# Attention's set-up copies move to the start, and the softmax sums and the product's copies move from VectorE to ScalarE

## The chip, the cores and the metric

The kernel runs on one core of a Trainium2 chip. A core has five engines that work side by side: TensorE (PE in the rows; its weight loads are PEld), VectorE (DVE), ScalarE (ACT), GpSimd (POOL) and SyncE (SP), which issues most of the transfers. Each engine takes its own instructions in order. The metric is the device time of one execution in microseconds, the median of several runs; lower is better. A profile shows a single execution.

## The reference

An attention over 4 batches of 8 heads feeds a mixture of experts (one expert for each token), and that feeds a gated product. Only the attention and the hand-over to the experts matter here.

```python
q_rot, k_rot = rotate(q), rotate(k)                 # 4 x 8 heads, 576 positions, 64 wide
scores = matmul(q_rot, k_rot^T) / 8
attn = exp(scores - max(scores))
attn = attn / (sum(attn) + 1e-9)
x = (attn @ v) -> [2304 tokens, 512]
logits = x @ w_gate                                  # chooses each token's expert
eom = sigmoid(x @ w_output_gate)
# then: experts with w1, w2; then gate * value @ w_out
```

## The kernel before

The 32 heads are taken as 16 pairs (g = 0 to 15), and the 576 queries of a pair in five pieces (j = 0 to 4, the last with 64 queries of both heads). One step t = 5g + j of the main loop writes out, for every engine in this order:

- scores(g, j): TensorE's products of queries and keys (L279, for j = 4 L274), VectorE's two negated row maxima (L285, tile nm), and ScalarE's two exponentials (L292, tile p), each followed by a short instruction that reads the row sum out of its accumulator. For j = 4 there is one maximum and one exponential.
- pv of step t-2: the product with the values (L339, L347) into the PSUM tile o. After j = 1 and j = 4 parts of o are copied to SBUF, to oT (256 columns after j = 1; 256 and 64 columns after j = 4). As pv runs two steps behind, the copies for j = 1 come in a step with j = 3, and those for j = 4 in a step with j = 1 of the next pair.
- turn_last and turn of step t-1: TensorE transposes the exponentials (L310, L325), VectorE copies one block (L311, tile pt), and ScalarE copies two pieces of 512 columns (L328, tile pt). The next step's pv reads pt.
- in steps with j = 3 and j = 4, xf(g-1): TensorE turns oT back to rows by a product with wI (L382). wI holds an identity matrix and beside it the two gates' weights, so that each row also gets its gate logits. VectorE divides by the softmax sum (L392 to L402). The sum of the last 64 queries, which lie in the two halves of the partitions, is brought together by a small product with the matrix fold (L390).
- for j = 0 to 2, tqk of the next pair: the transposes of its keys and queries (L241, L249), whose high and low parts VectorE writes (L230, L231). In pair 0's own set-up ScalarE writes the high parts (L228).

All transposes, xf's products and tqk's share three PSUM tiles (pool pst), and the scores two pairs of tiles (pool pss). A tile is free for its next user when its last reader is done. GpSimd rotates the pair after next (L193 to L208); of the first pair VectorE does it. In step 2 late_setup, and at the end of step 5 late_setup2, set up what xf and the choice of experts need: wI, fold, ones, tri, ids_tok and base.

Ahead of the loop the kernel turns the first pair's keys and queries. In the wait for them TensorE runs transposes of the identity whose results nobody reads ("spin", L221): 30 ahead of the keys' own and 8 ahead of the queries'.

Of the kernel before, what the change touches and what calls it, by code (L numbers as in the profile page):

```python
# [9 lines left out]
F32 = mybir.dt.float32  # L10
# [4 lines left out]
AF = mybir.ActivationFunctionType  # L15
ALU = mybir.AluOpType
# [27 lines left out]
XW = DM + 1  # L44
EPS = 1e-9
# [20 lines left out]
def tile_kernel(  # L66
# [16 lines left out]
    nc = tc.nc  # L83
# [38 lines left out]
    halves = mc[:, 280:282]  # L122
# [57 lines left out]
    rotd = {}  # L180
# [30 lines left out]

        return a, b

    def tqk(g, eng=nc.vector, spin=(0, 0, 0)):

        i = g % 2

        def place(n):
            ps = pst.tile([128, 512], F32, tag="t", name="t")
            for _ in range(spin[n]):  # L220
                nc.tensor.transpose(ps[:, 0:128], idf, idf)  # L221
            return ps

        def halves_of(hi, lo, ps, nm):

            f = SCALE if nm == "q" else 1.0
            if eng is nc.scalar:
                nc.scalar.activation(out=hi, in_=ps, func=AF.Copy, scale=f)  # L228
            else:
                nc.vector.tensor_scalar(out=hi, in0=ps, scalar1=f, scalar2=None, op0=ALU.mult)  # L230
            nc.vector.scalar_tensor_tensor(  # L231
                out=lo, in0=ps, scalar=f, in1=hi.bitcast(F32), op0=ALU.mult, op1=ALU.subtract
            )

        def main(nm):
            def f():
                src = rotd[g, nm]
                h, l = qT[i] if nm == "q" else (t[:, 64:576] for t in kT[i])
                ps = place("kq".index(nm))
                for c in range(4):  # L240
                    nc.tensor.transpose(ps[:, 128 * c : 128 * c + 128], src[:, c, :], idf)  # L241
                halves_of(h, l, ps, nm)

            return f

        def tails():
            ps = place(2)
            for n, nm in enumerate("kq"):
                nc.tensor.transpose(ps[:, 64 * n : 64 * n + 64], rotd.pop((g, nm))[0:64, 4, :], idf[0:64, 0:64])  # L249
            for c in (0, 576):  # L250
                halves_of(*(t[:, c : c + 64] for t in kT[i]), ps[:, 0:64], "k")
            for e in range(2):
                r = slice(64 * e, 64 * e + 64)
                halves_of(*(t[r, r] for t in qD[i]), ps[r, 64:128], "q")

        return [main("k"), main("q"), tails]

# [74 lines left out]
    def pv(g, j):  # L332
        if j == 0:
            OPS[g] = po.tile([128, 512], F32, tag="o", name="o")
        ps, src, (va, vd) = OPS[g], PT.pop((g, j)), vraw[g]
        q0, n = (128 * j, 128) if j < 4 else (0, 64)
        for c in range(4):
            for e in range(2):
                nc.tensor.matmul(  # L339
                    ps[64 * e : 64 * e + 64, q0 : q0 + n],  # L340
                    va[:, e, c, :],
                    src[:, 4 * e + c, :] if j < 4 else src[:, c, 64 * e : 64 * e + 64],
                    start=(c == 0),
                    stop=False,
                    skip_group_check=True,
                )
        nc.tensor.matmul(ps[:, q0 : q0 + n], vd, src[:, 8, 0:n], start=False, stop=True, skip_group_check=True)  # L347
        if j == 1:
            nc.vector.tensor_copy(O[g % 2][:, 0:256], ps[:, 0:256])
        elif j == 4:  # L350
            nc.vector.tensor_copy(O[g % 2][:, 256:512], ps[:, 256:512])
            nc.vector.tensor_copy(O[g % 2][:, 512:576], ps[:, 0:64])

# [9 lines left out]
    def xf(g):  # L365
# [4 lines left out]
        def part(c0, nch):  # L370
            def f():
                if c0 == 0:
                    st["r"] = sm.tile([128, 5, 2], F32, tag="r", name="r")
                    st["x"] = xp.tile([128, 5, 129], F32, tag="x", name="x")
                    sp = sm.tile([128, 2], F32, tag="sp", name="sp")
                    nc.vector.tensor_tensor(out=sp, in0=halves, in1=lst.pop(g).to_broadcast([128, 2]), op=ALU.mult)
                    st["sp"] = sp
                X, r = st["x"], st["r"][:, c0 : c0 + nch, :]
                ps = pst.tile([128, 512], F32, tag="t", name="t")
                for c in range(nch):  # L380
                    cc = c0 + c
                    nc.tensor.matmul(  # L382
                        ps[:, 160 * c : 160 * c + 160],
                        O[g % 2][:, 128 * cc : 128 * cc + 128],
                        wI[:, h, :],
                        start=True,
                        stop=True,
                    )
                if c0:
                    nc.tensor.matmul(ps[:, 320:322], fold, st["sp"], start=True, stop=True)  # L390
                    nc.vector.tensor_copy(l[:, 4, :], ps[:, 320:322])
                nc.vector.tensor_scalar(out=r, in0=l[:, c0 : c0 + nch, :], scalar1=EPS, scalar2=None, op0=ALU.add)  # L392
                nc.vector.reciprocal(out=r, in_=r)
                r = r.unsqueeze(3)
                pv_ = ps[:, 0 : 160 * nch].rearrange("p (c w) -> p c w", w=160)
                nc.vector.tensor_tensor(
# [587 lines left out]
        nc.vector.memset(t, 1.0)  # L984
    for t in (*(x.bitcast(F32) for x in (*qD[0], *qD[1])), *(vd for _, vd in vring + vlast)):
        nc.vector.memset(t, 0.0)
    load(1)
    load(0, "v")
    R = {nm: rot(0, nm) for nm in "kq"}
    for nm in "kq":  # L990
        for f in R[nm]:
            f(eng=nc.vector)
    first, gate_q = tqk(0, nc.scalar, (30, 8, 0)), rotd[0, "q"]
    for f in first:
        f()

    nc.gpsimd.tensor_copy(scr, gate_q[0:1, 0, 0:1])
    load(2)
# [4 lines left out]

    def late_setup():
        nc.sync.dma_start(out=mc, in_=misc)
        nc.gpsimd.memset(wI, 0.0)
        nc.gpsimd.memset(pinit, DUMMY)
        for t in O:
            nc.gpsimd.memset(t[:, 576:640], 0.0)
        nc.sync.dma_start(out=x_dram[0:1, :], in_=wI.rearrange("p h w -> p (h w)")[0:1, 0:XW])  # L1010
        for e in range(2):
            r = slice(64 * e, 64 * e + 64)
            for o, w in ((0, w_gate), (E, w_og)):
                c = 128 + 16 * e + o
                nc.sync.dma_start(
                    out=wI[r, :, c : c + E],
                    in_=w.rearrange("(h e p) n -> e p h n", h=4, e=2)[e],
                )

    def late_setup2():  # L1020
        nc.vector.tensor_copy(wI[:, :, 0:128], idf.unsqueeze(1).to_broadcast([128, 4, 128]))
        nc.vector.tensor_copy(tri, mc[:, 0:128])
        for o in range(2):
            nc.vector.tensor_tensor(
                out=fold[:, 64 * o : 64 * o + 64], in0=idf[:, 0:64], in1=idf[:, 64:128], op=ALU.add
            )
        nc.vector.memset(ones, 1.0)
        nc.vector.tensor_copy(ids_tok, mc[:, 128:148])
        nc.vector.tensor_copy(base, mc[:, 272:280])
        nc.sync.dma_start(out=perm_dram.rearrange("(p a) o -> p (a o)", p=128), in_=pinit)  # L1030

    M["seq"] = MAIN
# [9 lines left out]
    for t in range(NJ * NPAIR):  # L1042
        g, j = divmod(t, NJ)
        if t == NJ * (NPAIR - 1):
# [6 lines left out]
            gather(0)  # L1051
            gather(1)
        scores(g, j)
        if t >= 2:
            pv(*divmod(t - 2, NJ))
        if t >= 1:
# [316 lines left out]
```

## Time and profile before

| | before |
|---|---|
| median of 3 runs | 1128.62 us (1127.61 to 1129.76) |
| profiled execution | 1129.55 us, of which the span from first to last instruction is 1127.8 us |
| busy share of the span | PE 95%, PEld 85%, DVE 68%, ACT 52%, POOL 32% |
| TensorE clock granted, mean | 0.986 of full speed |
| attention's steps | from about 11 to 360 us |

A row of a timeline begins with the start and the duration in us, then engine, line of the kernel, operation, output<-input with the partitions and elements, the count, and in brackets how long the engine had been idle and what released it.

### The profile page before, as it was taken

The page shows a single profiled execution, that of the slowest core. Times are in us where ns is not written, and L with a number is a line of the kernel's source. Part 1 is how long each engine was busy: PE and PEld are TensorE (multiplying, and loading weights), DVE is VectorE, ACT ScalarE, POOL GpSimd, SP SyncE. Part 2 cuts the span into 40 slices and gives each one's busy share as a digit, 9 for nine tenths or more (in the row PEclk, how much of TensorE's full clock was granted, in tenths as well). Part 3 has the DMA queues.
Part 4 walks back from the last instruction along what each step waited for, and adds up shares of the span by engine and source line. Part 5 has one row for each costly group of instructions (what it writes and reads, how often), then busy time and mean ns, then how long its engine had stood idle before and what let it go on. Part 6 is the DMA issues. An engine that isn't in the chain of part 4 may idle for free. (4 is left out here: it accounts for less than half of the span.)

```text
span 1127.8 us, 20456 instructions
## 1 busy us (share of the span) xinstructions
PE 1076.3 (95%) x7682; PEld 961.7 (85%) x7682; DVE 771.9 (68%) x1439; ACT 582.2 (52%) x1122; POOL 360.3 (32%) x336
## 2 busy tenths in 40 slices
PE   7799998989998999999999999999999999999998
PEld 6688787778777988988888889888999999999997
DVE  6778787787876886889989868854444545444442
ACT  4466455555544344667667656654444444444432
POOL 6335454553612103444333134521111111111111
PEclk8899999999999999999999999999999999999999
DMA  4144045045008297699999543300010010100000
GB/s 112 37 84 77 12 50 102 9 56 87 30 14 227 48 146 267 197 330 301 324 302 318 200 142 122 103 1 28 1 57 1 10 47 1 57 1 1 28 1 28
DMA packets 97053, 111.61 MB, mean 99 GB/s; under 512 B 16817, under 2 KB 75441, under 8 KB 96946
## 3 DMA queue, kind: packets, MB, share of 16 engines
q1 hardware_dynamic: 92482, 97.81, 31.2%
q0 software_dynamic: 4320, 12.08, 3.7%
q8 instruction: 62, 1.02, 0.4%
q14 instruction: 45, 0.37, 0.1%
q10 hardware_dynamic: 144, 0.33, 0.1%
HBM read 103.03 MB, written 15.56 MB: 105 GB/s over the span
## 5 line engine op out<-in xcount | busy, mean ns | idle before, releaser
L1242 POOL TENSOR_TENSOR gl<-gf,gh 128x384 fp32r<-128x384 f32 x72 | 73.3, 1018 | 348.6 <-ACT gh L1241 348.6
L292 ACT ACTIVATE p<-s,nm 128x576 f32<-128x576 f32 x144 | 105.6, 738 | 125.8 <-DVE nm L285 121.4
L771 DVE TENSOR_TENSOR lo<-wr,hi 128x1024 fp32r<-128x1024 f32 x112 | 156.4, 1409 | 14.7 <-ACT hi L770 14.3
L1237 DVE TENSOR_TENSOR gf<-v,sg 128x384 f32<-128x384 f32 x72 | 40.0, 555 | 134.0 <-PE v L1233 134.0
L285 DVE TENSOR_REDUCE nm<-s 128x1 f32<-128x576 f32 x144 | 102.9, 751 | 39.2 <-PE s L279 26.0
L1241 ACT CAST gh<-gf 128x384 fp32r<-128x384 f32 x72 | 36.9, 513 | 160.5 <-DVE gf L1237 160.5
L1216 DVE TENSOR_TENSOR gl<-gw,gh 128x512 fp32r<-128x512 f32 x72 | 72.9, 1012 | 66.8 <-ACT gh L1215 66.7
L770 ACT CAST hi<-wr 128x1024 fp32r<-128x1024 f32 x106 | 109.7, 1052 | 5.4 <-PE y L861 2.7
L325 PE MATMUL t<-idf,p 128*128 128x128 f32 x576 | 84.4, 282 | 19.0 <-DVE pt L311 16.7
L1231 PE MATMUL t<-yh,gh 128*128 128x384 f32 x288 | 99.1, 344 | 1.8 <-ACT gh L1215 1.6
L1233 PE MATMUL t<-yh,gl 128*128 128x384 f32 x288 | 97.4, 338 | 0.6 <-DVE gl L1216 0.2
L1232 PE MATMUL t<-yl,gh 128*128 128x384 f32 x288 | 96.7, 336 | 0.0
L1233 PE MATMUL v<-yh,vl 128*128 128x384 f32 x288 | 96.2, 334 | 0.0
L1231 PE MATMUL v<-yh,vh 128*128 128x384 f32 x288 | 96.2, 334 | 0.0
L1232 PE MATMUL v<-yl,vh 128*128 128x384 f32 x288 | 96.2, 334 | 0.0
L328 ACT COPY pt<-t 128x512 f32<-128x512 f32 x144 | 79.2, 589 | 31.3 <-PE t L325 30.7
L325 PEld LDWEIGHTS t<-idf,p 128*128 128x128 f32 x576 | 67.1, 146 | 27.1 <-DVE pt L311 21.3
L830 PE MATMUL h<-xl,hi 128*128 128x256 f32 x288 | 82.0, 285 | 1.8 <-DVE sc L806 1.8
L830 PE MATMUL h<-xh,hi 128*128 128x256 f32 x288 | 81.9, 284 | 0.7 <-DVE hl L835 0.7
L830 PE MATMUL h<-xh,lo 128*128 128x256 f32 x288 | 81.5, 283 | 0.0
L1235 ACT ACTIVATE sg<-t 128x384 f32<-128x384 f32 x72 | 35.3, 491 | 81.8 <-PE t L1233 81.8
L861 PE MATMUL y<-hi,hl 128*128 128x512 f32 x184 | 73.0, 397 | 4.6 <-DVE hl L847 4.4
(235 smaller groups left out, 2974.8 us busy)
## 6 DMA issues: line engine op xcount, KB each, us to landing
wr<-in_moe_w_dram SPq DMA_DIRECT2D x112, 512.0 KB
cv<-in_moe_w_gate_dram SPq DMA_DIRECT2D x12, 512.0 KB
cv<-in_moe_w_val_dram SPq DMA_DIRECT2D x12, 512.0 KB
cv<-in_moe_w_out_dram SPq DMA_DIRECT2D x12, 512.0 KB
yt<-y_dram SPq DMA_DIRECT2D x18, 256.0 KB
out_dram<-ob SPq DMA_DIRECT2D x18, 256.0 KB
kraw<-in_k_dram SPq DMA_DIRECT2D x16, 256.0 KB
qraw<-in_q_dram SPq DMA_DIRECT2D x16, 256.0 KB
```

Source lines behind the costliest of these rows:

```text
L285: nc.vector.tensor_reduce(out=nm, in_=s[:, :, 0:288], axis=AX.XY, op=ALU.max, negate=True)
L292: nc.scalar.activation(out=P[g, j][:, e, :].rearrange("p (a b) -> p a b", a=2), in_=s[:, :, 0:288], func=AF.Exp, bias=nm, scale=1.0, accum ...
L325: nc.tensor.transpose(ps[:, 128 * c : 128 * c + 128], src[:, e, k0 + 128 * c : k0 + 128 * c + 128], idf)
L328: nc.scalar.copy(dst[:, 4 * e : 4 * e + 4, :].rearrange("p c q -> p (c q)"), ps)
L770: nc.scalar.copy(out=hi, in_=t)
L771: nc.vector.tensor_tensor(out=lo, in0=t, in1=hi.bitcast(F32), op=ALU.subtract)
L830: nc.tensor.matmul(ps[:, c, :], w[:, kk, 128 * c : 128 * c + 128], x[:, kk, :], start=first, stop=last)
L861: nc.tensor.matmul(ps, hl, rh, start=False, stop=False)
L1231: nc.tensor.matmul(ps[:, 0:TG], wh[:, c], yh[:, kk, :], start=(kk == 0), stop=False)
L1232: nc.tensor.matmul(ps[:, 0:TG], wh[:, c], yl[:, kk, :], start=False, stop=False)
L1233: nc.tensor.matmul(ps[:, 0:TG], wl[:, c], yh[:, kk, :], start=False, stop=(kk == KD - 1))
L1242: nc.gpsimd.tensor_tensor(out=gl, in0=gf, in1=gh.bitcast(F32), op=ALU.subtract)
```

## The change

1. wI's identity and zero columns and the matrix fold are made by VectorE ahead of the loop, behind its first memsets. late_setup2 keeps three copies out of mc (tri, ids_tok, base), now by ScalarE, and ones, now by GpSimd.
2. The first pair's set-up is reordered: the 64-column remainder ("tails") of the keys is turned behind the keys' main part, and that of the queries only after scores(0, 0). The dummy transposes are 30, 6 and 0, and 14 ahead of the queries' remainder.
3. The three copies of o to oT go from VectorE to ScalarE in every pair.
4. In xf, ScalarE makes sp (from the last sums) and writes the sums plus EPS into spare columns of the PSUM tile that the product with wI fills; VectorE takes the reciprocal from there. A multiplication, two additions and a copy leave VectorE for each pair, and a sum no longer goes by way of lsum.
5. The row of zeros at the head of x_dram is written from pinit by 27 partitions, no longer from wI.

```diff
@@ tqk @@
-    def tqk(g, eng=nc.vector, spin=(0, 0, 0)):
+    def tqk(g, eng=nc.vector, spin=(0, 0, 0, 0)):
...
-        def tails():
-            ps = place(2)
+        def tails(which="kq"):
+            ps = place(2 if "k" in which else 3)
             for n, nm in enumerate("kq"):
+                if nm not in which:
+                    continue
                 nc.tensor.transpose(ps[:, 64 * n : 64 * n + 64], rotd.pop((g, nm))[0:64, 4, :], idf[0:64, 0:64])
...
@@ pv @@
         if j == 1:
-            nc.vector.tensor_copy(O[g % 2][:, 0:256], ps[:, 0:256])
+            nc.scalar.copy(O[g % 2][:, 0:256], ps[:, 0:256])
         elif j == 4:
-            nc.vector.tensor_copy(O[g % 2][:, 256:512], ps[:, 256:512])
-            nc.vector.tensor_copy(O[g % 2][:, 512:576], ps[:, 0:64])
+            nc.scalar.copy(O[g % 2][:, 256:512], ps[:, 256:512])
+            nc.scalar.copy(O[g % 2][:, 512:576], ps[:, 0:64])
@@ xf @@
-                    nc.vector.tensor_tensor(out=sp, in0=halves, in1=lst.pop(g).to_broadcast([128, 2]), op=ALU.mult)
+                    nc.scalar.activation(out=sp, in_=halves, func=AF.Copy, scale=lst.pop(g))
...
+                e = ps[:, 480 : 480 + 2 * nch]
                 if c0:
                     nc.tensor.matmul(ps[:, 320:322], fold, st["sp"], start=True, stop=True)
-                    nc.vector.tensor_copy(l[:, 4, :], ps[:, 320:322])
-                nc.vector.tensor_scalar(out=r, in0=l[:, c0 : c0 + nch, :], scalar1=EPS, scalar2=None, op0=ALU.add)
-                nc.vector.reciprocal(out=r, in_=r)
+                    nc.scalar.activation(out=e[:, 0:2], in_=l[:, 3, :], func=AF.Copy, bias=EPS)
+                    nc.scalar.activation(out=e[:, 2:4], in_=ps[:, 320:322], func=AF.Copy, bias=EPS)
+                else:
+                    nc.scalar.activation(out=e.rearrange("p (c h) -> p c h", h=2), in_=l[:, 0:3, :], func=AF.Copy, bias=EPS)
+                nc.vector.reciprocal(out=r, in_=e.rearrange("p (c h) -> p c h", h=2))
@@ ahead of the loop @@
+    nc.vector.memset(wI[:, :, 128:160], 0.0)
+    nc.vector.tensor_copy(wI[:, :, 0:128], idf.unsqueeze(1).to_broadcast([128, 4, 128]))
+    for o in range(2):
+        nc.vector.tensor_tensor(out=fold[:, 64 * o : 64 * o + 64], in0=idf[:, 0:64], in1=idf[:, 64:128], op=ALU.add)
...
-    first, gate_q = tqk(0, nc.scalar, (30, 8, 0)), rotd[0, "q"]
-    for f in first:
-        f()
+    first, gate_q = tqk(0, nc.scalar, (30, 6, 0, 14)), rotd[0, "q"]
+    first[0]()
+    first[2]("k")
+    first[1]()
@@ late_setup @@
-        nc.gpsimd.memset(wI, 0.0)
...
-        nc.sync.dma_start(out=x_dram[0:1, :], in_=wI.rearrange("p h w -> p (h w)")[0:1, 0:XW])
+        nc.sync.dma_start(out=x_dram[0:1, :].rearrange("o (p c) -> (o p) c", p=27), in_=pinit[0:27, 0:19].bitcast(F32))
@@ late_setup2 @@
-        nc.vector.tensor_copy(wI[:, :, 0:128], idf.unsqueeze(1).to_broadcast([128, 4, 128]))
-        nc.vector.tensor_copy(tri, mc[:, 0:128])
-        for o in range(2):
...
-        nc.vector.memset(ones, 1.0)
-        nc.vector.tensor_copy(ids_tok, mc[:, 128:148])
-        nc.vector.tensor_copy(base, mc[:, 272:280])
+        nc.gpsimd.memset(ones, 1.0)
+        for o, c in ((tri, slice(0, 128)), (ids_tok, slice(128, 148)), (base, slice(272, 280))):
+            nc.scalar.copy(out=o, in_=mc[:, c])
@@ main loop @@
         scores(g, j)
+        if t == 0:
+            first[2]("q")
         if t >= 2:
             pv(*divmod(t - 2, NJ))
```

In the three places below the lines of the changed kernel are other numbers for the same code: L279 became L283, L285 L289, L292 L296, L311 L315, L328 L332, L349 to L352 became L353 to L356.

VectorE's list around the end of step 5 before (tile nm is the maximum, oT the copied product):

```order
L231 SCALAR_TENSOR_TENSOR kTl_150<-t,kTh_149 128x512
L1021 COPY wI<-idf 128x4x128
L1022 CAST tri<-mc 128x128
L1024 TENSOR_TENSOR fold<-idf 128x64 x2
L1027 MEMSET ones 128x128
L1028 CAST ids_tok<-mc 128x20
L1029 COPY base<-mc 128x8
L285 TENSOR_REDUCE nm<-s 128x1 x2
L351 COPY oT_154<-o 128x256
L352 COPY oT_154<-o 128x64
L311 COPY pt<-t 128x128
```

and the same place now:

```order
L231 SCALAR_TENSOR_TENSOR kTl_150<-t,kTh_149 128x512
L289 TENSOR_REDUCE nm<-s 128x1 x2
L315 COPY pt<-t 128x128
L230 TENSOR_SCALAR qTh_141<-t 128x512
L231 SCALAR_TENSOR_TENSOR qTl_142<-t,qTh_141 128x512
```

The six set-up rows and the two copies of oT are gone from between step 6's inputs and its maxima, and from between the maxima and the copy of pt.

ScalarE's list from a step with j = 1 to the next step with j = 4, in pair 2, before:

```order
L292 ACTIVATE p,lsum_156<-s,nm 128x576 x2
L328 COPY pt<-t 128x512 x2
L292 ACTIVATE p,lsum_156<-s,nm 128x576 x2
L328 COPY pt<-t 128x512 x2
L292 ACTIVATE p,lsum_156<-s,nm 128x576 x2
L328 COPY pt<-t 128x512 x2
L292 ACTIVATE p,lst<-s,nm 128x576
L328 COPY pt<-t 128x512 x2
```

and now, from behind the exponentials of the step with j = 1:

```order
L355 COPY oT_155<-o 128x256
L356 COPY oT_155<-o 128x64
L332 COPY pt<-t 128x512 x2
L296 ACTIVATE p,lsum_156<-s,nm 128x576 x2
L332 COPY pt<-t 128x512 x2
L296 ACTIVATE p,lsum_156<-s,nm 128x576 x2
L353 COPY oT_154<-o 128x256
L380 ACTIVATE sp<-mc,lst 128x2
L400 ACTIVATE t<-lsum_156 128x6
L332 COPY pt<-t 128x512 x2
L296 ACTIVATE p,lst<-s,nm 128x576
L397 ACTIVATE t<-lsum_156 128x2
```

Two copies (j = 1), a copy and two small activations (j = 3) and two small activations (j = 4; the second, L398, is the next row) now stand between the exponentials and the two copies of pt.

TensorE's list at the program's start, before:

```order
L221 MATMUL t<-idf 128x128 x30
L241 MATMUL t<-idf,trk 128x128 x4
L221 MATMUL t<-idf 128x128 x8
L241 MATMUL t<-idf,trq 128x128 x4
L249 MATMUL t<-idf,trk 128x64
L249 MATMUL t<-idf,trq 128x64
L279 MATMUL s<-kTh_149,qTh_141 128x288 x2
```

and now:

```order
L221 MATMUL t<-idf 128x128 x30
L241 MATMUL t<-idf,trk 128x128 x4
L251 MATMUL t<-idf,trk 128x64
L221 MATMUL t<-idf 128x128 x6
L241 MATMUL t<-idf,trq 128x128 x4
L283 MATMUL s<-kTh_149,qTh_141 128x288 x2
```

and, also now, at the end of the first step's scores and the beginning of the second's:

```order
L283 MATMUL s<-kTh_149,qTl_142 128x288 x2
L283 MATMUL s<-kTl_150,qTh_141 128x288 x2
L221 MATMUL t<-idf 128x128 x14
L251 MATMUL t<-idf,trq 128x64
L283 MATMUL s<-kTh_149,qTh_141 128x288 x2
```

The keys' remainder comes ahead of the queries' wait, and the 14 dummy transposes with the queries' remainder stand between the first and the second step's scores.

## Rows read from the trace of the kernel before

**Rows 1.** Windows: PE, PEld, DVE, ACT, POOL busy us (instructions), clock, DMA share, GB/s.
```profile
50.00:100.00 50.00, 49.59 (x538) 43.00 (x537) 38.58 (x103) 30.10 (x69) 18.72 (x16) 1.00 0.27 55
```
**Rows 2.** Page, part 2: granted clock in tenths, 40 slices of 28 us.
```profile
PEclk8899999999999999999999999999999999999999
```
**Rows 3.** Timeline, steps 6 and 7.
```profile
36.51 1.48 DVE L1021 COPY wI<-idf 128x512 f32<-128x512 f32 x1
...
38.70 2.38 DVE L1024 TENSOR_TENSOR fold<-idf 128x64 f32<-128x64 f32 x2
...
41.83 1.41 DVE L285 TENSOR_REDUCE nm<-s 128x1 f32<-128x576 f32 x2
...
43.96 1.12 PE L325 MATMUL t<-idf,p 128*128 128x128 f32 x4 [5.92 <-DVE pt L311]
...
46.74 1.30 PE L339 MATMUL o<-pt,v 128*64 128x128 f32 x16
```
**Rows 4.** Waits of TensorE, 30 to 430 us: total us, times, longest.
```profile
PE t L325 <- DVE pt L311: 16.7, 18, 5.9
```
**Rows 5.** Timeline, step 11 (pair 2, j = 1) up to step 12's pv.
```profile
62.66 1.41 DVE L285 TENSOR_REDUCE nm<-s 128x1 f32<-128x576 f32 x2
...
64.78 0.66 PE L325 MATMUL t<-idf,p 128*128 128x128 f32 x4 [0.21 <-DVE pt L311]
64.86 0.20 ACT L292 ACTIVATION_READ_ACCUMULATOR p<-s,nm 128x1 f32 x1
64.95 1.12 ACT L328 COPY pt<-t 128x512 f32<-128x512 f32 x2
...
66.37 1.09 PE L339 MATMUL o<-pt,v 128*64 128x128 f32 x16
```
**Rows 6.** Timeline, step 13 (j = 3) up to step 14's pv.
```profile
73.17 1.07 ACT L328 COPY pt<-t 128x512 f32<-128x512 f32 x2 [0.46 <-PE t L325]
...
74.23 1.15 PE L339 MATMUL o<-pt,v 128*64 128x128 f32 x16
```
**Rows 7.** Groups by line, ScalarE, 48 to 350 us: busy us, mean ns of one.
```profile
L328 ACT COPY pt<-t 128x512 f32<-128x512 f32 x128 | 70.4, 589 | 28.4 <-PE t L325 28.0
L292 ACT ACTIVATION_READ_ACCUMULATOR p<-s,nm 128x1 f32 x128 | 25.0, 196 | 0.0
```
**Rows 8.** Timeline, the start.
```profile
5.08 0.82 DVE L193 TENSOR_TENSOR ta<-kraw,ropes 128x640 f32<-128x640 f32 x1 [2.54 <-DMA kraw<-in_k_dram]
...
10.03 0.18 POOL L997 COPY scr<-trq 1x1 f32<-1x1 f32 x1 [7.70 <-DVE trq L208]
...
12.84 0.30 PE L279 MATMUL s<-kTl,qTh 64*128 64x288 f32 x2
...
13.72 1.42 DVE L285 TENSOR_REDUCE nm<-s 128x1 f32<-128x576 f32 x2
...
15.40 1.32 PE L279 MATMUL s<-kTh,qTh 64*128 64x288 f32 x2 [2.27 <-ACT p L292]
```
**Rows 9.** Timeline, one VectorE product of 128x40 twice, and GpSimd beside the first.
```profile
124.51 1.55 POOL L208 TENSOR_TENSOR trk<-ta,tb 128x640 f32<-128x640 f32 x1
...
124.69 1.43 DVE L452 TENSOR_TENSOR val<-val,mc 128x40 f32<-128x40 f32 x1
...
383.24 0.19 DVE L452 TENSOR_TENSOR val<-val,mc 128x40 f32<-128x40 f32 x1
```
**Rows 10.** Groups by line, dummy transposes' weight loads, 2.3 to 6 and 6.3 to 9 us.
```profile
L221 PEld LDWEIGHTS t<-idf 128*128 128x128 f32 x18 | 3.7, 227 | 2.4 <-POOL idf masks.py:199 2.4
...
L221 PEld LDWEIGHTS t<-idf 128*128 128x128 f32 x19 | 2.1, 141 | 0.0
```
**Rows 11.** Timeline, step 9 (j = 4).
```profile
57.73 1.07 ACT L328 COPY pt<-t 128x512 f32<-128x512 f32 x2 [1.13 <-PE t L325]
```
**Rows 12.** Timeline, steps 37 and 56, two long waits.
```profile
171.28 1.42 DVE L285 TENSOR_REDUCE nm<-s 128x1 f32<-128x576 f32 x2 [3.88 <-remote]
...
251.96 1.33 PE L279 MATMUL s<-kTh,qTh 64*128 64x288 f32 x2 [2.21 <-issue]
```

More of the change, by code (lines that the diff above doesn't have):

```diff
@@ L244, in main @@
             return f
-        def tails():
-            ps = place(2)
+        def tails(which="kq"):
+            ps = place(2 if "k" in which else 3)
             for n, nm in enumerate("kq"):
+                if nm not in which:
+                    continue
                 nc.tensor.transpose(ps[:, 64 * n : 64 * n + 64], rotd.pop((g, nm))[0:64, 4, :], idf[0:64, 0:64])
[L250 to L254, printed above, removed]
+            if "k" in which:
+                for c in (0, 576):
+                    halves_of(*(t[:, c : c + 64] for t in kT[i]), ps[:, 0:64], "k")
+            if "q" in which:
+                for e in range(2):
+                    r = slice(64 * e, 64 * e + 64)
+                    halves_of(*(t[r, r] for t in qD[i]), ps[r, 64:128], "q")
         return [main("k"), main("q"), tails]
@@ L1020, in late_setup2 @@
     def late_setup2():
-        nc.vector.tensor_copy(wI[:, :, 0:128], idf.unsqueeze(1).to_broadcast([128, 4, 128]))
-        nc.vector.tensor_copy(tri, mc[:, 0:128])
-        for o in range(2):
-            nc.vector.tensor_tensor(
-                out=fold[:, 64 * o : 64 * o + 64], in0=idf[:, 0:64], in1=idf[:, 64:128], op=ALU.add
-            )
-        nc.vector.memset(ones, 1.0)
-        nc.vector.tensor_copy(ids_tok, mc[:, 128:148])
-        nc.vector.tensor_copy(base, mc[:, 272:280])
+        nc.gpsimd.memset(ones, 1.0)
+        for o, c in ((tri, slice(0, 128)), (ids_tok, slice(128, 148)), (base, slice(272, 280))):
+            nc.scalar.copy(out=o, in_=mc[:, c])
         nc.sync.dma_start(out=perm_dram.rearrange("(p a) o -> p (a o)", p=128), in_=pinit)
```

## The prediction

> **What bounds the kernel now.** I read the windows of the attention first. Between 50 and 100 us TensorE is busy 49.59 of 50 us at full clock, while VectorE is busy 38.6 and ScalarE 30.1 [rows 1]. So an edit gains there only where TensorE visibly waits. The slices of the page come next: the granted clock shows an 8 in the first two slices and a 9 in all others [rows 2], so the lost clock lies in the first 56 us. The timeline there shows the one large hole of the attention: TensorE idle for 5.92 us at 43.96, released by the copy of pt on VectorE [rows 3]. The list of waits puts this in proportion: TensorE waited 18 times for that copy, 16.7 us in all, 5.9 of them here; the other 17 waits make 10.8 us, 0.6 us each [rows 4].
>
> What happens in the hole: at the end of step 5 VectorE begins the set-up copies at 36.51 and reaches step 6's maxima only at 41.83 [rows 3]. The exponentials wait for the maxima, the copy of pt stands behind them, TensorE's next transposes need the tile that this copy frees. The work behind the hole then runs at the lower clock: step 7's 16 products with the values take 1.30 us, against 1.09 in a regular step [rows 3, 5].
>
> In the regular steps TensorE and ScalarE are tied to each other: pv of the next step starts at 66.37, 0.30 us after ScalarE's copies of pt end (64.95 + 1.12), and at 74.23 it starts as they end (73.17 + 1.07) [rows 5, 6]. What the change puts ahead of these copies on ScalarE is therefore the question that decides it.
>
> **The hole (term 1).** Without the set-up, step 6's maxima start at 36.51 in place of 41.83. From the maxima of a regular step with j = 1 to the next pv it takes 66.37 - 62.66 = 3.71 us [rows 5]. So step 7's pv comes at 40.2 in place of 46.74: 6.5 us gained [rows 3]. The slow clock on that pv's products (1.30 against 1.09) gives back 0.2 more. Together 6.7. The three copies from mc that ScalarE takes over stand behind the copies of pt of step 5, where ScalarE in the old program had nothing to do until the exponential that followed the 41.83 maxima; ones on GpSimd lies beside that. I cost these at nothing; without that cover they would delay step 6's exponentials by three short instructions of 0.2 us [rows 7], 0.6 us.
>
> **The set-up in its new place (term 2).** VectorE stands idle 2.54 us before the first keys come at 5.08 [rows 8]. There the memset, the copy of wI and the two sums of fold must fit. At the durations of the old place (1.48 and 2.38 us) they would need 4 us and be 1.5 us late [rows 3]. But a 128x40 product on VectorE takes 1.43 us while GpSimd works beside it and 0.19 us in another place [rows 9], and GpSimd stands idle for 7.70 us until 10.03 [rows 8]. A wide operation from SBUF takes 0.82 us for 640 columns there [rows 8], so about 0.65 for 512, and with three short ones of 0.19 about 1.2 us in all. That fits, so 0; bounds 0 and +1.5.
>
> **The start (term 3).** The first maxima start at 13.72, although the scores that they read end at 13.14 (12.84 + 0.30) [rows 8]: the remainders of keys and queries stand between on VectorE. Now the keys' remainder is done in the wait for the queries, and the queries' comes behind these maxima. So the chain of the first step moves up by 0.6 us. Against it, 14 dummy transposes stand ahead of the second step's scores, which start at 15.40 after a wait of 2.27 us [rows 8]. With loads of 141 ns one behind the other the 14 take 2.0 us, with 227 ns 3.2 us [rows 10]: from 13.14 they end at 15.1 or at 16.3. If the clock holds they hide and may save slow-clock time; if it doesn't, they cost up to 0.9 beyond 15.40. I take a gain of 0.6; the bounds are -1.2 (as much again from slow-clock time) and +0.9.
>
> Whether dummy transposes hold the clock is disputed. While TensorE ran nothing but transposes, its weight loads went from 227 to 141 ns [rows 10], so here they raised the clock. The Trainium skill ("TensorE: Matmul & The Clock Gate", Part 4, PE-mode transpose) says that the full clock does not engage for transposes, which would not count as a busy TensorE. By that rule the start would gain nothing, and the sum below would be 0.6 us smaller. The trace disagrees with it.
>
> **The copies of oT, j = 1 (term 4).** In this step TensorE waits 0.21 us for the copy of pt, which stands behind the two copies of oT on VectorE [rows 5]. That wait goes, but the two copies now stand on ScalarE ahead of the copies of pt. The trace shows no such ScalarE copy, so I work between two rows: 589 ns for 512 columns and 196 ns for one [rows 7]. That gives 0.39 us for 256 columns and 0.24 for 64. A following instruction starts about 0.1 us before the end of the one ahead (64.86 + 0.20, next start 64.95) [rows 5], so in the queue they cost 0.29 + 0.14 = 0.43. The copies of pt then start at 65.38 and end 1.07 later at 66.45, and pv comes at 66.45 in place of 66.37: 0.1 us lost where 0.2 seemed to be won. Fifteen such steps: +1.5. If each costs its full duration, pv comes at 66.65: +0.28 a step. If ScalarE hides them, pv is held only by TensorE: -0.21 a step.
>
> **The copy of oT and the sums, j = 3 (term 5).** ScalarE is idle 0.46 us ahead of the copies of pt [rows 6], with the overlap of 0.1 there is room for 0.56. Put in are 0.29 for the copy and twice 0.1 for the short activations (196 ns with 0.1 overlap), 0.49: it fits, 0. With full durations, 0.39 + 0.2 + 0.2 = 0.79, it costs 0.33 a step. VectorE's reciprocal then waits for ScalarE, and the next step's single maximum stands behind xf's two products on VectorE; that next step (j = 4) has 1.13 us of idle ScalarE ahead of its copies [rows 11], which covers it.
>
> **The sums, j = 4 (term 6).** Two short activations in those 1.13 us [rows 11]: 0. They start only when the product with fold is done, shortly before the transposes; the bounds are 0 and 0.2. For the first and the last pairs, whose steps are less regular, I add 0.4 in all from the bounds of term 5.
>
> **The choice of experts (term 7).** The 10.8 us in the 17 other waits [rows 4] lie largely in steps in which VectorE also works on the choice of experts. The copy of pt comes earlier by the copies of oT there too, but pv is then held by ScalarE, as in term 4. I take 1.0 us of gain; bounds 0 and 5.
>
> **Sum.** -6.7 + 0 - 0.6 + 1.5 + 0 + 0.4 - 1.0 = -6.4 us. The profiled execution took 1129.55, 0.93 above the median of the runs, so it would go to 1123.2 and the median from 1128.62 to 1122.2. Nothing behind the attention has a start of its own: its loads are issued from the attention's steps, so I pass the gain through whole.
>
> **Rivals.**
> - *ScalarE becomes the bound, even.* At full durations terms 4 and 5 cost 0.61 for each of 15 pairs, 9.2 us in place of 1.9: the sum is +0.9, 1129.5. For it: the two engines meet with 0.0 to 0.3 us between them [rows 5, 6]. Against: the measured overlap of 0.1.
> - *ScalarE becomes the bound, slower.* If besides each of the three inserted instructions that wait for another engine pays a hand-over as long as the shortest instruction (0.2) [rows 7], a pair costs 1.2 us, 18 us in all: 1138. It decides for slower from 0.71 us a pair. Against: the copies' inputs are ready before ScalarE is.
> - *Two unexplained waits move.* VectorE stood 3.88 us at 171.28 and TensorE 2.21 us at 251.96 for nothing that the profile names [rows 12]; I estimate 4 to 5 us for each, the wait and the slower clock behind it. ScalarE's and VectorE's lists get other lengths, so such waits may fall elsewhere: one or both gone, 1117.5 or 1113; one more, 1126.7.
> - *The set-up does not fit at the start.* 1123.7, inside the forecast's range.
>
> **Chances and range.** Forecast 0.58, with a range of its own from 1119 to 1126; ScalarE even 0.10; ScalarE slower 0.09; waits gone 0.13; one more 0.10. The range from 1115 to 1129 leaves out most of the slower case, both waits gone, and little else. A measurement can tell about 0.2% from no change, 2.3 us. Below 1126.4 lie the forecast, the waits gone and part of the case with one more: 0.74. Within 2.3 us: 0.15. Above: 0.11.
>
> **What would show it.** Right: VectorE's maxima of step 6 near 36.5 and no hole of TensorE beyond 0.6 us there; step 7's pv near 40; pv in steps with j = 2 and 4 starting right as ScalarE's copies of pt end. Wrong: distances between pv's in a regular pair that grow by over 0.5 us; a first use of the keys later than 5.1 us; dummy transposes that end after 15.4; long waits at other places than 171 and 252 us.

## The result, and the profile after

The changed kernel took 1120.41 us in the median (1117.56 to 1121.26, 4 runs) against 1128.57 (1127.61 to 1129.76): a ratio of 0.9914, 95% interval 0.9892 to 0.9936. The forecast was 1122.2, with 1115 to 1129 as its range. The profiled execution took 1120.27 us, with a span of 1118.5.

The page's first part gives each engine's busy time, its second the granted clock in 40 slices of 28 us. The two slices with an 8 [rows 2] are gone, and 30 us of VectorE's work (771.9 before). A 9 stands for 90% or more; the profile's mean clock went from 0.986 to 0.994.

```profile
PE 1078.1 (96%) x7694; PEld 963.9 (86%) x7694; DVE 741.6 (66%) x1324; ACT 601.0 (54%) x1237; POOL 360.5 (32%) x336
...
PEclk9999999999999999999999999999999999999999
```

The timeline of steps 6 and 7 answers to [rows 3]: step 6's maxima start at 35.42, straight behind the keys' low part (L231), TensorE runs through, and the products with the values start at 35.31 in step 6 and at 38.86 in step 7.

```profile
34.81 0.69 DVE L231 SCALAR_TENSOR_TENSOR kTl<-t,kTh 128x512 fp32r<-128x512 f32 x1
...
35.31 0.69 PE L343 MATMUL o<-pt,v 128*64 128x64 f32 x16
35.42 1.41 DVE L289 TENSOR_REDUCE nm<-s 128x1 f32<-128x576 f32 x2
...
36.75 1.04 PE L329 MATMUL t<-idf,p 128*128 128x128 f32 x8
...
38.86 1.44 PE L343 MATMUL o<-pt,v 128*64 128x128 f32 x16
```

In the kernel before, step 6's products stand here:

```profile
36.00 0.69 PE L339 MATMUL o<-pt,v 128*64 128x64 f32 x16
```

TensorE's waits from 30 to 430 us (total, times, longest) answer to [rows 4]. Of 16.7 us behind the copy of pt 3.5 are left; the hole was 5.9 of the 13.2 that went.

```profile
PE t L329 <- DVE pt L315: 3.5, 5, 1.3
```

The start, beside [rows 8]: the copy of wI and the sums of fold take VectorE 0.6 us in their new place, and VectorE then stands idle for 2.23 us until the keys are there. Between the first step's scores and the second's, TensorE now runs dummies.

```profile
2.59 0.36 DVE L996 COPY wI<-idf 128x512 f32<-128x512 f32 x1
2.86 0.34 DVE L998 TENSOR_TENSOR fold<-idf 128x64 f32<-128x64 f32 x2
5.44 0.82 DVE L193 TENSOR_TENSOR ta<-kraw,ropes 128x640 f32<-128x640 f32 x1 [2.23 <-DMA kraw<-in_k_dram]
...
13.45 1.75 PE L221 MATMUL t<-idf 128*128 128x128 f32 x14
13.54 1.42 DVE L289 TENSOR_REDUCE nm<-s 128x1 f32<-128x576 f32 x2 [1.02 <-PE s L283]
...
20.29 1.09 PE L343 MATMUL o<-pt,v 128*64 128x128 f32 x16
```

Step 11 (j = 1), beside [rows 5]: the copies of oT stand ahead of those of pt on ScalarE and put them off by 0.35 us (57.12 to 57.47).

```profile
57.02 0.20 ACT L296 ACTIVATION_READ_ACCUMULATOR p<-s,nm 128x1 f32 x1
57.12 0.37 ACT L355 COPY oT<-o 128x256 f32<-128x256 f32 x1
57.37 0.23 ACT L356 COPY oT<-o 128x64 f32<-128x64 f32 x1
57.47 1.10 ACT L332 COPY pt<-t 128x512 f32<-128x512 f32 x2
...
58.26 1.45 PE L343 MATMUL o<-pt,v 128*64 128x128 f32 x16
...
77.66 1.45 PE L343 MATMUL o<-pt,v 128*64 128x128 f32 x16
```

The products with the values now start 0.31 us ahead of the end of the copies (57.47 + 1.10) and take 1.45 us in place of 1.09. From pair to pair they stand 77.66 - 58.26 = 19.40 us apart.

The two long waits of [rows 12] have moved, not gone. TensorE waits 2.26 us in step 36 and 2.09 us at 242.

```profile
156.91 0.40 PE L283 MATMUL s<-kTh,qTh 64*128 64x288 f32 x1 [2.26 <-ACT p L296]
...
242.41 0.40 PE L283 MATMUL s<-kTh,qTh 64*128 64x288 f32 x1 [2.09 <-issue]
```

### The profile page after: what moved, and what is told of

It reads as the page before. It is cut to its first block, busy times and chain, and to the rows that moved or that the text cites. A ratio compares the mean times of both kernels' runs of the same rounds, so it can differ in the third digit from the quotient of the medians.

```text
span 1118.5 us, 20352 instructions
## 1 busy us (share of the span) xinstructions
PE 1078.1 (96%) x7694; PEld 963.9 (86%) x7694; DVE 741.6 (66%) x1324; ACT 601.0 (54%) x1237; POOL 360.5 (32%) x336
## 5 line engine op out<-in xcount | busy, mean ns | idle before, releaser
L779 DVE TENSOR_TENSOR lo<-wr,hi 128x1024 fp32r<-128x1024 f32 x112 | 156.1, 1407 | 16.3 <-ACT hi L778 15.8
L296 ACT ACTIVATE p<-s,nm 128x576 f32<-128x576 f32 x144 | 105.5, 737 | 100.9 <-DVE nm L289 96.9
L289 DVE TENSOR_REDUCE nm<-s 128x1 f32<-128x576 f32 x144 | 102.8, 751 | 29.2 <-PE s L283 23.3
L332 ACT COPY pt<-t 128x512 f32<-128x512 f32 x144 | 78.9, 597 | 15.4 <-PE t L329 13.9
L329 PE MATMUL t<-idf,p 128*128 128x128 f32 x576 | 80.5, 278 | 5.6 <-DVE pt L315 3.5
L343 PE MATMUL o<-pt,v 128*64 128x128 f32 (+1 forms) x1120 | 77.0, 272 | 0.3
```

The costliest lines, as they stand in the source:

```text
L289: nc.vector.tensor_reduce(out=nm, in_=s[:, :, 0:288], axis=AX.XY, op=ALU.max, negate=True)
L296: nc.scalar.activation(out=P[g, j][:, e, :].rearrange("p (a b) -> p a b", a=2), in_=s[:, :, 0:288], func=AF.Exp, bias=nm, scale=1.0, accum ...
L329: nc.tensor.transpose(ps[:, 128 * c : 128 * c + 128], src[:, e, k0 + 128 * c : k0 + 128 * c + 128], idf)
L332: nc.scalar.copy(dst[:, 4 * e : 4 * e + 4, :].rearrange("p c q -> p (c q)"), ps)
L343: nc.tensor.matmul(ps[64 * e : 64 * e + 64, q0 : q0 + n], va[:, e, c, :], src[:, 4 * e + c, :] if j < 4 else src[:, c, 64 * e : 64 * e + 6 ...
L779: nc.vector.tensor_tensor(out=lo, in0=t, in1=hi.bitcast(F32), op=ALU.subtract)
```

## The experiments

Each ratio is to the kernel before in runs on the same chip; the chips differ (medians of before: 1126.5 for the first four kernels, 1123.31 and 1122.06 on another chip for the rest), so a time is compared only with those of runs beside it on the same chip.

**Each part alone.** The first: only part 1 of the change, the set-up moved.

```diff
+    nc.vector.tensor_copy(wI[:, :, 0:128], idf.unsqueeze(1).to_broadcast([128, 4, 128]))
...
-        nc.vector.tensor_copy(wI[:, :, 0:128], idf.unsqueeze(1).to_broadcast([128, 4, 128]))
-        nc.vector.tensor_copy(tri, mc[:, 0:128])
...
+            nc.scalar.copy(out=o, in_=mc[:, c])
```

> The kernel before, with the set-up of the gates' matrix and of fold moved to the wait for the first keys and the copies from mc on ScalarE; nothing else changed. Theory (the hole is the gain, and the moves to ScalarE give the rest in the choice of experts): TensorE's hole between steps 6 and 7 goes, step 7's products with the values start near 39.6 in place of 46.74, all later steps of the plain pairs 7.2 us early, and the steps with the choice of experts keep that distance: about 1121.4 us, 1123 if some of it is given back behind the attention. Rival (the set-up does not fit in the wait): the first use of the keys is later than 5.1 and the time is 1122.9. Rival (the gain in the experts' steps comes from other places of the instruction lists, not from the relief of VectorE): these steps gain some us here too, 1115 to 1118.

Measured: 1119.01 us, 0.9943 (0.9929 to 0.9957), 0.6% less than before. Step 7's products with the values start at 40.02, and the first keys are used at 5.09, so the set-up fits where it was put. The hole alone brings the greater part of the result.

The second: only parts 3 and 4, the moves to ScalarE.

```diff
-            nc.vector.tensor_copy(O[g % 2][:, 0:256], ps[:, 0:256])
+            nc.scalar.copy(O[g % 2][:, 0:256], ps[:, 0:256])
...
+                    nc.scalar.activation(out=e[:, 2:4], in_=ps[:, 320:322], func=AF.Copy, bias=EPS)
```

> The kernel before, with only the copies of oT and the short operations on the sums moved from VectorE to ScalarE. Theory: plain pairs keep their 19.40 us to within 0.1, the hole of step 6 stays, and the steps with the choice of experts become about 6 us shorter in all, because VectorE comes earlier to the copy of pt: 1122.6 at the attention's end, 1124 to 1126 if some is given back behind it. Rival (ScalarE is at the end of its room): a plain pair grows by 0.1 to 0.7 us, 1130 to 1138. Rival (the moves are worth nothing anywhere, the experts' steps shifted by chance): 1128.6.

Measured: 1128.3 us, 1.0019 (1.0006 to 1.0032). In the attention TensorE's waits for the copy of pt fell as expected (10.3 us in place of 16.7, of them 5.5 in the hole), but its products with the values now waited 3.7 us for ScalarE's copies, which they did not before. The whole took a little more time. That was missed.

The third: only part 2, the first step reordered and the dummies. The set-up stays in step 5 on VectorE.

```diff
-    first, gate_q = tqk(0, nc.scalar, (30, 8, 0)), rotd[0, "q"]
+    first, gate_q = tqk(0, nc.scalar, (30, 6, 0, 14)), rotd[0, "q"]
...
+        if t == 0:
+            first[2]("q")
```

> The kernel before, with only the first step reordered: the keys' remainder ahead of the queries, the queries' behind the first scores, 14 dummy transposes ahead of the second step. Theory: step 2's products with the values start 0.8 us early, the hole of step 6 stays (its length is set by VectorE's set-up, which moves with the start): 1127.8. Rival (dummy transposes neither hold the clock nor hide): 1128.6 to 1129.5.

Measured: 1121.5 us, 0.9957 (0.9935 to 0.9979): 5 us where 0.8 were expected. Both expectations were wrong, and the trace of one execution (1122.51 us; the twelve lie between 1116.5 and 1126.51) says why. The timeline of VectorE and GpSimd around the set-up, which stands where it stood before, with the same instructions:

```profile
35.10 0.42 DVE L1026 COPY wI<-idf 128x512 f32<-128x512 f32 x1
35.43 0.22 DVE L1027 CAST tri<-mc 128x128 bf16<-128x128 f32 x1
35.57 0.35 DVE L1029 TENSOR_TENSOR fold<-idf 128x64 f32<-128x64 f32 x2
...
36.06 1.42 DVE L289 TENSOR_REDUCE nm<-s 128x1 f32<-128x576 f32 x2
36.26 1.53 POOL L193 TENSOR_TENSOR ta<-kraw,ropes 128x640 f32<-128x640 f32 x1 [6.35 <-DMA kraw<-in_k_dram]
...
38.20 0.66 PE L329 MATMUL t<-idf,p 128*128 128x128 f32 x4 [1.40 <-DVE pt L315]
```

The copy of wI takes 0.42 us where it took 1.48 [rows 3], both sums of fold 0.35 in place of 2.38, and the whole set-up 0.96 us (35.10 to 36.06) in place of 5.32 (36.51 to 41.83). The difference is GpSimd: here its rotations start 0.2 us behind the set-up, in the kernel before they started 0.35 us ahead of it (36.16 against 36.51 [rows 3]), and the cast of tri took 0.87 us where it now takes 0.22. From the kernel before:

```profile
36.16 1.55 POOL L193 TENSOR_TENSOR ta<-kraw,ropes 128x640 f32<-128x640 f32 x1 [6.20 <-DMA kraw<-in_k_dram]
...
37.91 0.87 DVE L1022 CAST tri<-mc 128x128 bf16<-128x128 f32 x1
```

So most of the hole was not work of the set-up but its collision with GpSimd: 4.4 of the 5.3 us. The maxima, which read PSUM, take 1.41 to 1.42 us with the rotations beside them or without. This is what the Trainium skill ("SBUF — State Buffer", Who interferes with whom) says of it: VectorE's copies and casts in their two-port modes and its operations with two inputs from SBUF share a pair of ports with GpSimd, whoever comes first holds it, and a reduction never contends. The traces agree in kind: copy, cast and sum grew beside a rotation that had begun ahead of the set-up, the maxima didn't.

The fourth: the changed kernel without the moves to ScalarE, parts 1, 2 and 5 alone.

```diff
-            nc.scalar.copy(O[g % 2][:, 0:256], ps[:, 0:256])
+            nc.vector.tensor_copy(O[g % 2][:, 0:256], ps[:, 0:256])
...
-                    nc.scalar.activation(out=sp, in_=halves, func=AF.Copy, scale=lst.pop(g))
+                    nc.vector.tensor_tensor(out=sp, in0=halves, in1=lst.pop(g).to_broadcast([128, 2]), op=ALU.mult)
```

> The changed kernel without both moves to ScalarE: the set-up and the first step as changed, the copies of oT and the sums on VectorE as before. Theory: step 7's products start near 38.9, plain pairs take 19.40 us, the experts' steps take what they took before: 7.9 us less than before, 1120.7, and the changed kernel would be some 4 to 6 us ahead at the attention's end. Rival (the gain of the moves to ScalarE is lost again behind the attention): the two kernels take the same time, 1120.4, though the attention of this one ends later. Rival (the moves to ScalarE cost time): this kernel is faster than the changed one, 1118 or less.

Measured: 1120.01 us, 0.9949 (0.9931 to 0.9968). Parts 1 and 2 do not add up (0.9943 and 0.9957 each alone): in the traces either of them removes most of the same hole.

**The collision, and the changed kernel on this chip.** The changed kernel was run again unchanged beside the next three.

> The changed kernel itself once more, on the same chip as the next three. In the runs so far the set-up alone took 0.9943 of the kernel before and the version without the moves to ScalarE 0.9949, while the changed kernel had 0.9914 in other runs. Theory (the moves to ScalarE gain some 3 us in the steps with the choice of experts and lose about as much behind the attention, so they are worth nothing in the end): 0.994 to 0.996 of the kernel before. Rival (the moves to ScalarE are worth the difference of 0.3%): 0.991 to 0.992.

Measured: 1111.97 us, 0.9897 (0.9882 to 0.9912), below both ranges. It speaks against the theory that the moves are worth nothing, but across chips; the last four versions below test it on one.

To test the collision by itself, the kernel before with one number changed: the set-up is called a step earlier, when GpSimd has nothing to do, and stays VectorE's.

```diff
-        if t == 5:
+        if t == 4:
             late_setup2()
```

> The kernel before with the same set-up on VectorE by the same instructions, called in step 4 in place of step 5, so that VectorE runs it before GpSimd starts its rotations at about 36 us. Theory (the hole is no work of the set-up but its collision with GpSimd): the six copies take 1.0 us in all in place of 5.3, the hole between steps 6 and 7 goes, step 7's products with the values start near 40, and the time is that of the set-up moved to the start, 0.994 of before, with none of the work taken off VectorE. Rival (the set-up is too much for VectorE in any step of the attention): a hole of 4 to 5 us stands between steps 5 and 6, and the time is that of before.

Measured: 1115.54 us, 0.9929 (0.9916 to 0.9943). In its timeline the set-up takes 1.10 us (33.28 to 34.38) ahead of GpSimd's start, and TensorE's longest wait there is 0.33 us:

```profile
33.28 0.43 DVE L1021 COPY wI<-idf 128x512 f32<-128x512 f32 x1
33.62 0.22 DVE L1022 CAST tri<-mc 128x128 bf16<-128x128 f32 x1
33.76 0.35 DVE L1024 TENSOR_TENSOR fold<-idf 128x64 f32<-128x64 f32 x2
...
34.38 1.42 DVE L285 TENSOR_REDUCE nm<-s 128x1 f32<-128x576 f32 x2
...
36.84 0.40 PE L279 MATMUL s<-kTh,qTh 64*128 64x288 f32 x1 [0.33 <-ACT p L292]
...
37.33 1.55 POOL L193 TENSOR_TENSOR ta<-kraw,ropes 128x640 f32<-128x640 f32 x1 [7.17 <-DMA kraw<-in_k_dram]
```

A single digit gives as much as moving the set-up to the start (0.9943, on the other chip), with no work taken from VectorE. Together with the third version, where the set-up kept its step and GpSimd came later, that shows the cause of the hole.

**The dummies.** The changed kernel without its 14 dummy transposes.

```diff
-    first, gate_q = tqk(0, nc.scalar, (30, 6, 0, 14)), rotd[0, "q"]
+    first, gate_q = tqk(0, nc.scalar, (30, 6, 0, 0)), rotd[0, "q"]
```

> The changed kernel without the 14 dummy transposes of the first step; nothing else changed. Theory (they hold TensorE's clock while it waits for the first exponentials): the granted clock falls in the first 20 us as in the kernel before (0.83 to 0.91 there against 1.00), step 2's products with the values start 0.3 to 0.8 us later, and the time is 0.5 to 1.5 us longer than the changed kernel's. Rival (dummy transposes count for nothing with the clock): clock and time as the changed kernel's. Rival (they stand in the way of the second step's scores): step 2 starts earlier and the time is shorter by up to 0.9 us.

Measured: 1112.89 us, 0.9902 (0.9887 to 0.9917), 0.9 us more than the changed kernel beside it; the intervals overlap. Step 2's products with the values come at 21.44 in place of 20.10, of which 0.24 us are a later arrival of the keys.

The granted clock is at half from about 13 to 19.7 us here, and stays full in the changed kernel. But it fell (0.94 from 12 to 13 us, 0.50 from 13 to 14) ahead of the place of the dummies, which start at 13.25 in the changed kernel, so their absence can't be what made it fall. What they do is told by the other versions. All five traces without them (before, the first two, the set-up in step 4, and this one) have a clock of 0.50 to 0.53 from 15 to 20 us. Of the nine with them, seven have 1.00 from 10 to 20 us. The other two are the two traces without the moves to ScalarE: there the clock fell ahead of the dummies as well, and came back while TensorE ran them. Windows (PE busy, granted clock, DMA share, GB/s) of the second of these two (neither move, the last four versions below), with its dummies:

```profile
13.00:16.00 3.00, 3.00 (x17) 0.50 0.67 190
16.00:20.00 4.00, 3.07 (x26) 0.96 0.03 5
...
13.30 3.19 PE L221 MATMUL t<-idf 128*128 128x128 f32 x14
```

and of the version without dummies:

```profile
13.00:16.00 3.00, 1.39 (x12) 0.50 0.72 205
16.00:20.00 4.00, 3.88 (x21) 0.54 0.00 1
```

The rule that transposes don't count for the clock (the Trainium skill, "TensorE: Matmul & The Clock Gate", Part 4) does not come out of these traces: the clock rose while the fp32 dummy transposes ran. Whether they run in the transpose mode that is meant there, no row shows.

**ScalarE's room.** The changed kernel with every copy of oT made twice.

```diff
         if j == 1:
-            nc.scalar.copy(O[g % 2][:, 0:256], ps[:, 0:256])
+            for _ in range(2):
+                nc.scalar.copy(O[g % 2][:, 0:256], ps[:, 0:256])
...
```

> The changed kernel with each copy of oT on ScalarE made twice (the second writes the same values). Theory (ScalarE has room left in the steps with j = 1 and j = 3, since in the changed kernel the products with the values no longer wait for the end of the copies of pt): a plain pair grows by 0 to 0.2 us, up to 3 us in all. Rival (ScalarE stands at the end of its room): the second copies come on top in full, 0.4 us at j = 1 and 0.3 at j = 3 in each of 16 pairs, 11 us in all.

Measured: 1121.38 us, 0.9985 (0.9975 to 0.9995), 9.4 us more than the changed kernel. The rival was right, though its 11 us were somewhat high. The timeline of a step with j = 1: the second copies put those of pt off by 0.37 us more, and TensorE now waits for them in the open. A plain pair takes 79.60 - 59.43 = 20.17 us in place of 19.40.

```profile
58.00 0.37 ACT L357 COPY oT<-o 128x256 f32<-128x256 f32 x1
58.25 0.23 ACT L358 COPY oT<-o 128x64 f32<-128x64 f32 x1
58.40 0.37 ACT L357 COPY oT<-o 128x256 f32<-128x256 f32 x1
58.67 0.22 ACT L358 COPY oT<-o 128x64 f32<-128x64 f32 x1
58.77 1.09 ACT L332 COPY pt<-t 128x512 f32<-128x512 f32 x2
...
59.43 1.58 PE L343 MATMUL o<-pt,v 128*64 128x128 f32 x16 [0.22 <-ACT pt L332]
...
79.60 1.58 PE L343 MATMUL o<-pt,v 128*64 128x128 f32 x16 [0.21 <-ACT pt L332]
```

**Which move is worth something.** Four versions side by side on one chip: none, one or both of the moves to ScalarE, all else as in the changed kernel.

```diff
@@ copies_only: part 4 undone @@
-                    nc.scalar.activation(out=e[:, 0:2], in_=l[:, 3, :], func=AF.Copy, bias=EPS)
...
+                nc.vector.tensor_scalar(out=r, in0=l[:, c0 : c0 + nch, :], scalar1=EPS, scalar2=None, op0=ALU.add)
...
@@ sums_only: part 3 undone @@
-            nc.scalar.copy(O[g % 2][:, 0:256], ps[:, 0:256])
+            nc.vector.tensor_copy(O[g % 2][:, 0:256], ps[:, 0:256])
...
```

> The version without both moves to ScalarE once more, on one chip with the next three. So far it had 0.9949 of the kernel before on one chip and the changed kernel 0.9897 and 0.9914 on two others, so the worth of the moves was read across chips. Theory (once the hole is gone the moves to ScalarE are worth some 3 to 6 us, by the relief of VectorE in the steps with the choice of experts): 0.993 to 0.995. Rival (they are worth nothing, and the difference was the chip's): within 0.1% of the changed kernel in this call.

> The changed kernel with the copies of oT on ScalarE, but the short operations on the sums on VectorE as before. Theory (the worth goes with the VectorE time that a move saves: 1.24 us of each pair by the copies, some 0.45 by the sums): three quarters of the gain of both, 0.991 to 0.992 of before. Rival (the copies take from ScalarE what they give VectorE, as doubling them costs 0.8 us a pair): no better than the version without both moves, 0.993 to 0.995.

> The changed kernel with the short operations on the sums on ScalarE, through the sums' copy in PSUM, but the copies of oT on VectorE as before. Theory: a quarter of the gain of both moves, 0.993 to 0.994 of before. Rival (each short activation waits for the product with fold and holds the copies of pt behind it on ScalarE): a pair grows by 0.1 to 0.3 us and the time is above that of the version without both moves, 0.996 to 0.998.

> The changed kernel again, as the fourth of this call. Theory: 0.990 to 0.9915 of before, 3 to 6 us less than the version without both moves. Rival (the moves are worth nothing): as that version.

Measured, with TensorE's waits for the copy of pt between 30 and 430 us in each trace:

| version | us | ratio to before | waits for pt: us, times, longest |
|---|---|---|---|
| neither move | 1115.77 | 0.9944 (0.9932 to 0.9956) | 8.1, 15, 1.8 |
| copies of oT | 1110.85 | 0.9904 (0.9891 to 0.9917) | 3.0, 5, 1.3 |
| sums | 1116.02 | 0.9945 (0.9932 to 0.9958) | 12.9, 16, 5.7 |
| both (the change) | 1112.29 | 0.9911 (0.9898 to 0.9924) | 3.6, 5, 1.4 |

By the medians the copies bring 4.9 us (the theory gave them three quarters of the gain; here they have all of it), and the sums nothing that can be told. The wait of 5.7 us in the version with the sums lies in the last pair, where VectorE stood 6.04 us for an expert's weights ahead of its maxima, so it says nothing of the sums; up to step 78 that version stands 1.2 us ahead of the one with neither move, 0.8 of them from step 2 on. The version with the copies alone is the fastest, but not apart from the changed kernel.

Where the copies' gain arises is shown only in part. Ten of the fifteen waits go with them, 5.1 us, but six of the ten are 0.2 us each in the regular rhythm, where they cost nothing (a plain pair takes 19.40 us without the copies on ScalarE and 19.49 with them). The version with the copies stands 2.3 us ahead of the one with neither move at the attention's last products (step 81: 352.23 against 354.56), and 0.7 of this stands already at step 2, where the clock of neither move had fallen. The changed kernel is 1.6 us ahead at step 78 and 0.2 at step 81 (354.37). The rest of the difference was not followed; the profiled execution of neither move (1113.43 us) was the fastest of its six.

## Why the prediction was right, and where it wasn't

It came out 1.8 us too high, and that it came so close is partly luck: two errors stand against each other. The hole and the start (terms 1 to 3) were put at -7.3 us; the version with these parts alone measured -6.3 (1115.77 against 1122.06). The moves to ScalarE (terms 4 to 7) were put at +0.9; beside it on the same chip they measured -3.5 (1112.29 against 1115.77). On that chip the whole sum was 3.4 us too high.

- *Term 1, the hole.* The size was right: from step 6's products to step 7's it takes 38.86 - 35.31 = 3.55 us in place of 46.74 - 36.00 = 10.74, 7.2 us less against 6.7. The reason was half of it: I counted the set-up's length as its work. Rows 9 were used for the set-up's new place and not for the old, where they said the same: 4.4 of the 5.3 us were GpSimd's.
- *Term 2.* Right: 0.6 us for wI and fold, and 2.23 us of idle VectorE behind them. The first use of the keys at 5.44 in place of 5.08 looks like the sign named for wrong, but it waits for their transfer; with the set-up alone moved it stands at 5.09.
- *Term 3.* Right in size, but largely by another way. Step 2's products come 0.83 us early (20.29 in place of 21.12), put at 0.6. From the first use of the keys to the first maxima it takes 8.10 us in place of 8.64 (5.44 to 13.54, 5.08 to 13.72), which is the 0.6 of the forecast; but the keys came 0.36 us later, so the maxima gained only 0.18. The rest goes with the clock, which was 1.00 from 15 to 20 us in place of 0.51. The dummies end at 15.20, inside the bound. On top of the set-up's move the new start can't be told from nothing in the time: 0.9949 with both, 0.9943 with the set-up alone.
- *Terms 4 to 6.* Too dear: a plain pair takes 19.40 us as before (85.78 - 66.37 = 19.41). The failed step is "pv comes as ScalarE's copies end". The products start when the first copy is done, 0.31 us ahead of that end, and take 0.36 us longer, waiting inside. Their end, 59.71, is that of before (67.46) less the 7.76 us that step 13's products stand earlier (70.20 to 62.44): the 0.30 us between copies and products in [rows 5] paid for the copies of oT. Doubling them showed that nothing is left of it.
- *Term 7, the choice of experts.* The mis-sized term, as far as is known: 1.0, with 5 as the bound. The waits outside the hole went from 10.8 us to 3.5, and the copies of oT alone took 5.1 us of such waits, of which some 1.6 us arrive at the attention's end. Where VectorE comes last and not ScalarE, the argument of term 4 does not carry over; that this makes up the whole 3.5 us is not shown.
- *The slices.* "So the lost clock lies in the first 56 us" was read too far, as a 9 hides up to a tenth. The first 56.4 us have a mean clock of 0.88, which loses 6.8 us; the whole span has 0.986, which loses 15.8. Ten-microsecond windows from 170, 250, 320 and 350 us show 0.83, 0.66, 0.83 and 0.83. No term rests on it.
- *"I pass the gain through whole"* failed in the profiled execution. Its lead was 13.8 us at step 80's products, and 9.3 are left in the span. Two stretches at a lower clock lie there (windows: PE, PEld, DVE, ACT, POOL busy, clock); the changed kernel's last profile has 1.00 in both:

```profile
420.00:440.00 20.00, 19.12 (x124) 17.63 (x125) 10.90 (x17) 8.92 (x12) 5.27 (x5) 0.91 0.56 203
640.00:660.00 20.00, 17.55 (x89) 15.84 (x88) 12.40 (x20) 8.25 (x18) 3.68 (x3) 0.91 0.42 140
```

- *Rivals.* ScalarE as the bound lies one further copy away, as the doubled copies show. The unexplained waits moved, and of the four, two before and two now, three can be read. Ahead of the wait of 2.26 us VectorE spends 3.55 us on a 128x5 operation, which took 0.16 to 0.19 us in all four places of the kernel before, until GpSimd's two rotations are done; ahead of that of 2.09 us the same operation takes 3.37.

```profile
150.93 0.90 POOL L517 DMA_INDIRECT perm_dram<-ids_tok,pi  x1 [0.22 <-issue]
151.38 3.55 DVE L539 TENSOR_SCALAR den<-den 128x5 f32<-128x5 f32 x1
151.86 1.54 POOL L208 TENSOR_TENSOR trk<-ta,tb 128x640 f32<-128x640 f32 x1
153.36 1.54 POOL L208 TENSOR_TENSOR trq<-ta,tb 128x640 f32<-128x640 f32 x1
...
155.28 1.38 DVE L289 TENSOR_REDUCE nm<-s 128x1 f32<-128x576 f32 x2
...
237.06 3.37 DVE L539 TENSOR_SCALAR den<-den 128x5 f32<-128x5 f32 x1
```

The kernel before has the same ahead of its wait of 2.21 us at 251.96 [rows 12], on the operation that follows it on VectorE, which takes 0.15 to 0.17 us in its other three places; GpSimd's rotations stand at 247.06 and 248.56:

```profile
246.44 3.69 DVE L535 SCALAR_TENSOR_TENSOR den<-zs,den 128x5 f32<-128x5 f32 x1
```

So one of the two waits that the prediction called unexplained was such a collision, and the changed kernel has two of them.

What stays open: why the moves to ScalarE alone took 0.2% more while the hole was there, and 0.3% less when it was gone. There is no trace of the kernel before from those chips. The wait of 3.88 us in [rows 12] is not explained either, and a version without the collisions at 151 and 237 us was not tried.

## What to carry to other kernels

When an instruction takes several times what its shape takes elsewhere in the same trace, look at GpSimd in that stretch before counting it as work: moving it by a step may bring most of the gain. An engine that looks free by its busy share (ScalarE 54%) can stand at its limit in one step of the loop; doubling the suspected instruction shows it in one run. A move that costs nothing in the regular steps can still be worth something elsewhere, but a total of waits does not say how much: measure each move by itself (5.1 us of waits went with the copies here, and some 1.6 us arrived at the attention's end).

## What the runs showed of the hardware

- A collision with GpSimd stands in the trace as a long instruction, not as a wait: 0.22 us became 0.87 (cast of 128x128), 0.42 became 1.48 (copy of 128x512), 0.16 became 3.55 (128x5). The last one lasted over two GpSimd rotations, one right behind the other. When it began, GpSimd was still in an indirect transfer (150.93 to 151.83), so which of the two came first the trace does not tell.
- VectorE's copies out of PSUM kept their time beside the same rotations: oT took 0.41 us at 43.16 in the kernel before, and 0.40 to 0.43 in all sixteen pairs.
- How such a collision falls hangs on tenths of a microsecond: GpSimd's start depends on a transfer and came between 34.5 and 37.3 us in these traces, and the set-up, where it stood in step 5 on VectorE, began between 35.1 and 37.5.
- A run's time goes with its granted clock even within one kernel: with the first step alone reordered, 1116.5 us came with a mean clock of 0.999 and 1126.51 with 0.988. On the chip of the doubled copies the mean over the runs was 0.988 for the kernel before and 0.997 for the changed one, so part of what was gained goes with clock that no longer falls; how much of it is cause and how much consequence of the shorter waits was not separated.
- A copy of 128x256 from PSUM takes ScalarE 369 ns and one of 128x64 231 ns, but in the queue they put the next instruction off by 0.25 and 0.10 us.
